# TensorE transposes for the first tokens, a second batch of loads behind them, and a re-weighted order of work in a two-layer attention and FFN kernel

## The chip, the cores and the metric

The kernel runs on one core of one Trainium2 chip. The metric is device time in microseconds. A core has five engines that run their own instruction streams and meet at semaphores: TensorE (PE, matmuls; its weight loads are listed apart as PEld), VectorE (DVE), ScalarE (ACT), GpSimd (POOL) and SyncE (SP, which here only issues DMAs). ACT and POOL issue some DMAs as well.

## The reference

There are 2048 tokens of width 512 in bf16. Two layers follow each other with the same weights; each is an attention block and a gated FFN, both behind a LayerNorm without weights and both added to x:

```python
x = A_x
for _ in range(2):                       # written out in the reference
    x = x + A(layernorm(x), wq, wk, wv, wo, beta)
    x = x + B(layernorm(x), w1, w3, w2)

def A(x):                                # 32 heads of 16; 4 segments of 512 tokens
    q, k, v = x @ wq, x @ wk, x @ wv
    M, z = 0, 0
    for s in range(4):
        p = softmax(qs ks^T / 4 + causal mask)      # within the segment
        a_dot = p vs
        a_mem = (phi(qs) M) / (phi(qs) z + 1e-6)    # phi(t) = t+1 if t>0 else exp(t)
        o = sigmoid(beta) a_mem + (1 - sigmoid(beta)) a_dot
        M, z = M + phi(ks)^T vs, z + sum(phi(ks))
    return o @ wo

def B(x):                                # inner width 1376
    return (silu(x @ w1) * (x @ w3)) @ w2
```

The memory M is carried from segment to segment of a layer. For segment 0 it is zero, so the kernel skips its read there.

## The kernel before

**Work units.** Token tiles have 128 rows, a segment has four of them, and both layers together have eight segments, numbered g = 0 to 7 (g = 4 * layer + s). For a segment, `layer_norm` computes statistics on DVE (L541, L543), the power -0.5 on POOL (L548) and the normalized tile on DVE (L554), and turns each tile with a DMA transpose on SP (L558). `project` makes q and k transposed and v by rows, in twelve jobs of four matmuls (L593, L598); for the first segment q and k are made in two halves of 256 tokens. `attention` runs 20 units of logits (L766), Exp on ACT (L775) and causal masks on POOL (L788); `attend` multiplies by v (L814), copies the result from PSUM to an `xs` buffer and turns it with a DMA transpose (L826). `normalise` scales by the row sums, adds the memory part and transposes once more (L850 to L871). `out_proj` (L879, L883) adds to x, a second `layer_norm` follows, and `ffn` runs the gate and up matmuls (L910), tanh on ACT (L921), two products on DVE (L923, L927) and the down matmuls (L938) with their addition to x (L943). Segment 0 does its attention in two halves of 256 tokens.

`memory_update` forms phi(k)^T v (L657), adds it into `macc` (L663) and masks it into the block-diagonal `mblk` (L665). `memory_read` multiplies phi(q) with it: a denominator (`mden`, L680), its eps, reciprocal and gate on DVE (`mde` L685, L687, L688), and four numerators (`mnum`, L699) that DVE scales to `om` (L703).

**The order.** No order is written out by hand. Every operation is entered with the tiles it reads and writes, the buffers it uses, a priority (smaller goes first) and gates, which are operations that must have been issued before. A planner in the kernel's own Python, `Sched.schedule`, simulates the engines with estimated durations and fixes each engine's instruction order; the engines then run it strictly in that order. For each engine it takes the operations whose predecessors are issued and chooses by these lines:

```python
w = max(tf, s + (R_SLACK if op.mode == "R" else SLACK[e]))
...
lim = max(smin, tf) + LOOK[e]
```

`s` is the time at which the operand is estimated ready, `tf` the time at which the engine is free; among operations whose `w` lies within `LOOK` of the earliest, the smallest priority goes first. So `SLACK` is a margin by which an operand should be ready ahead, and `LOOK` is how far the engine may be kept for something more important. `DMA_SLACK` is an extra margin for DVE and TensorE behind a DMA. An operation that ends with several engines to choose from (`ev`, a copy from PSUM) goes to ACT or DVE, whichever starts first.

**Buffers.** PSUM has two pairs of banks for logits ("S") and four single banks ("B") for everything else. There are three `xs` buffers, eleven large "W" buffers for activations and two for the memory block.

**Head.** Warm-up matmuls on a zeroed buffer (`spin`, L472) keep TensorE running: eight operations, the first two planned as twice as long, 32 matmuls in all. SP and ACT issue the first loads (x tile 0, wq, x tile 2 on SP; x tile 1, wk, x tile 3, wv and beta on ACT). `second_loads` issues x tiles 4 to 7 and four pieces of w1 and w3 on SP behind the last transpose of the first LayerNorm; `late_loads` puts wo, x tiles 8 to 11, w2 and x tiles 12 to 15 on POOL's queue, each at a numbered attention unit of segment 0. `gate_constants` computes sigmoid(beta) by a tanh on ACT.

Of the kernel before, what the change touches and what calls it, by code (L numbers as in the profile page):

```python
# [4 lines left out]
ALU = mybir.AluOpType  # L5
# [22 lines left out]
DMA_SLACK = 800.0  # L28
# [4 lines left out]
SLACK = {"pe": 120.0, "act": 0.0, "dve": 200.0, "pool": 60.0, "sp": 0.0}  # L33
LOOK = {"pe": 90.0, "act": 100.0, "dve": 20.0, "pool": 20.0, "sp": 20.0}
# [29 lines left out]
class Sched:  # L64
# [59 lines left out]
    def schedule(self):  # L124
# [23 lines left out]
        while left:  # L148
# [88 lines left out]
            else:  # L237
# [7 lines left out]
                else:  # L245
                    x0 = max(s + 700.0, dma_free)
# [109 lines left out]
def build(nc, A_x, A_wq, A_wk, A_wv, A_wo, A_beta, B_w1, B_w3, B_w2, out):  # L356
# [33 lines left out]
    xs_r = ring("xs", 3, [P, 512])  # L390
# [11 lines left out]
    bdm = sb("bdm", [P, 8, 17])  # L402
    cm = [sb("cm%d" % i, [P, 1], F32) for i in range(2)]
# [37 lines left out]
    def ev(dst, src, n, **k):  # L441

        def fn(e):
            if hasattr(e, "activation"):
# [11 lines left out]
                                   base=15, channel_multiplier=-1), 136, reads=["bdm"], writes=["bdm"], prio=CP)  # L456
    for ee in range(2):
        dve(lambda e, ee=ee: e.tensor_reduce(cm[ee][:], bdm[:, ee::2, 0], axis=mybir.AxisListType.X, op=ALU.add), 4,
            reads=["bdm"], writes=["cm%d" % ee], prio=CP)
# [6 lines left out]
    WARM = 8  # L466
    if WARM:
        dve(lambda e: e.memset(xs_r[0][:], 0.0), 200, writes=["warm"], prio=CP - 1)

        def spin(e, B=new("B")):  # L470
            for _ in range(4):
                o = e.matmul(bank(B), xs_r[0][:, 0:128], xs_r[0][:], start=True, stop=True)  # L472
            return o
        wb = spin.__defaults__[0]
        pools["xs"].prev[0] = [pe(spin, 4 * MM512 * (2 if i < 2 else 1), reads=["warm"], writes=[(wb, 0)], bufs=[wb], prio=CP, name="warm")
# [22 lines left out]

    def second_loads(first):
        ldw("act", wv_sb, A_wv, "wv", CP + 3)  # L500
        rs = [op for op in S.ops[first:] if op.name == "xT"][-1]

        def early(out_ap, in_ap, size, n, keys, name):
            dma("sp", out_ap, in_ap, size, prio=CP + 4 + n, writes=keys, name=name, gates=[rs], after=[rs])
        early(x_tok[:, 4:8, :], xv[:, 4:8, :], 524288, 0, [("x", 4 + j) for j in range(4)], "ldx")
        for a in range(2):
            for n, (t, src, key) in enumerate(((w1_sb, B_w1, "w1"), (w3_sb, B_w3, "w3"))):
                early(t[:, 2 * a:2 * a + 2, :], src[256 * a:256 * a + 256, :].rearrange("(g p) f -> p g f", p=P), 704512,
                      2 + 2 * a + n, [key + str(a)], "ld" + key)
# [4 lines left out]
    def late_loads():  # L514
        for a in range(2):
            late(wo_sb[:, 2 * a:2 * a + 2, :], A_wo[256 * a:256 * a + 256, :].rearrange("(g p) f -> p g f", p=P), 262144,
                 5 + 2 * a, ["wo%d" % a], "ldwo")
        late(x_tok[:, 8:12, :], xv[:, 8:12, :], 524288, 9, [("x", 8 + j) for j in range(4)], "ldx")
# [5 lines left out]
        late(x_tok[:, 12:16, :], xv[:, 12:16, :], 524288, 18, [("x", 12 + j) for j in range(4)], "ldx")  # L524

    def gate_constants():
        act(lambda e: e.activation(gth[:], betab[:], ACT.Tanh, scale=0.5), 32, False, reads=["betab"], writes=["gth"], prio=0.1)
# [3 lines left out]
            reads=["gth"], writes=["g1"], prio=0.1)  # L531


    def layer_norm(s, name, prio, gates=(), fine=False, part=(0, LT), dst=None):
# [16 lines left out]
        for i in tiles:  # L551
# [5 lines left out]
                bufs=[st, xn], hold=[dst], prio=prio, name="norm")  # L557
            dmaT(lambda e, i=i, xn=xn: e.dma_start_transpose(dt_[dst.slot][:, :, i * 128:(i + 1) * 128], xn_r[xn.slot][:, :]),  # L558
# [4 lines left out]
    def release(g, n):  # L563
# [3 lines left out]
        return units.get((g - 2, 12 + n)) if n < 8 else units.get((g - 1, 2 * (n - 8)))  # L567
# [4 lines left out]
    def project(s, g, X, first):  # L572
# [10 lines left out]
        for n, (kind, Gs, hf) in enumerate(jobs):  # L583
# [36 lines left out]
            elif kind == "k" and Gs[0] == NCG - 1:  # L620
                for pg in range(4):
# [3 lines left out]
                          bufs=[z.k, z.km], prio=g - 1 + 0.3, name="km", gates=[units.get((g - 1, 4))])  # L625
# [17 lines left out]
    def memory_update(g, z, pkb):  # L643
# [5 lines left out]
        for hf in range(2):  # L649
            B = new("B")  # L650

            def fn(e, hf=hf, B=B):
# [11 lines left out]
                reads=[(B, 0), ("macc", hf)], writes=[("macc", hf)], bufs=[B], prio=g - 99.7, name="macc")  # L664
# [3 lines left out]
                375, reads=[("macc", hf), "bdm"], writes=[(mb, hf)], bufs=[mb], prio=g + 0.3, name="mblk")  # L668
        mstate["mb"] = mb

    def memory_read(g, pqb):
# [4 lines left out]
        def fn(e):  # L676
# [9 lines left out]
            writes=[(rm, 0)], bufs=[B, rm], prio=g - 99.9, name="mde")  # L686
# [333 lines left out]
```

## Time and profile before

| | us |
|---|---|
| median of 16 runs | 517.04 |
| lowest and highest of them | 516.23, 521.86 |
| the profiled execution, its own time | 516.87 |
| its span, first to last instruction | 515.1 |

Mean granted TensorE clock over the span: 0.980 of full speed.

How to read what follows. A row of an engine names the line of the kernel, the operation, what it writes and reads, and how many instructions it merges; in square brackets stands the idle time of that engine just ahead and what ended it. A row of stages gives, for each engine, busy time and instructions in brackets. Matmuls of one stream overlap, so the mean duration of one (about 380 ns at 512 columns) is longer than the distance from one to the next (about 215 ns). DMA transposes are issued one after another by SP.

| row of the groups | count | mean ns |
|---|---|---|
| Exp, L775 (ACT) | 180 | 1707 |
| PSUM copy, L445 (ACT) / L446 (DVE) | 55 / 105 | about 600 / 680 |
| mask, L788 (POOL) | 256 | 660 |
| memory numerator matmul 128x128, L699 (PE) | 96 | 223 |
| table load (ACT) | 1 | 1283 |
| DMA transposes of normalized tiles, L558 (SP), issue to landing | 64 | 2500 |

### The profile page before, as it was taken

To read this page: it belongs to the slowest core of one execution; us is meant where nothing else is said; L and a number is where in the kernel's file an instruction comes from. 1 tells how busy PE (TensorE), PEld (TensorE's weight loads), DVE (VectorE), ACT (ScalarE), POOL (GpSimd) and SP (SyncE) were. 2 spreads that over 40 slices of the span, in tenths; PEclk is the share of its full clock that TensorE was granted. 3 is DMA by queue.
4 is the path that set the end of the run, shared out by engine and by line. 5 is a ranking of instruction groups with operands and counts; after the bars stand their busy time and mean duration, and the time that the engine had idled before them with its cause. 6 is when DMAs were issued, how large, how long until landed. Compare 5 with 4: busy or idle time off the path is not lost.

```text
span 515.1 us, 10399 instructions
## 1 busy us (share of the span) xinstructions
PE 486.3 (94%) x4117; PEld 215.8 (42%) x4184; DVE 403.3 (78%) x809; ACT 395.9 (77%) x350; POOL 230.5 (45%) x340
## 2 busy tenths in 40 slices
PE   9978889999999999999799999999999999999997
PEld 4523434654543443334343344433433334444443
DVE  5786999985888798688956899869886597479472
ACT  1998999989978988789977999878988799522130
POOL 1676445564446545555433453454554454310000
PEclk9986999999999999999989999999999999999999
DMA  6969732441142254130531124213322122210201
GB/s 194 280 146 174 144 72 57 68 94 40 33 73 56 49 93 73 31 74 12 98 67 42 41 53 94 62 32 54 84 50 42 42 65 50 73 31 11 72 1 41
DMA packets 108144, 36.91 MB, mean 72 GB/s; under 512 B 101344, under 2 KB 105952, under 8 KB 108096
## 3 DMA queue, kind: packets, MB, share of 16 engines
q1 hardware_dynamic: 105728, 31.94, 30.1%
q0 software_dynamic: 880, 2.98, 2.2%
q10 hardware_dynamic: 1488, 1.32, 0.8%
q8 instruction: 33, 0.54, 0.5%
q14 instruction: 15, 0.12, 0.1%
HBM read 8.43 MB, written 2.10 MB: 20 GB/s over the span
## 4 chain that ended last, share of the span: by engine, by line
PE 66%; DVE 17%; ACT 12%; issue 2%; DMA 1%; POOL 0%
PE psall L910 25%; PE psall L938 15%; ACT e L775 10%; PE psall L766 7%; PE psall L814 6%; PE psall L598 6%; PE psall L879 4%; DVE xn L554 3%; DVE ln L541 2%; PE psall L472 2%; DVE h L927 2%; DVE gp L923 2%; PE psall L593 2%; ACT px L633 1%; DVE x_tok L883 1%
## 5 line engine op out<-in xcount | busy, mean ns | idle before, releaser
L775 ACT ACTIVATE e<-psall 128x2048 bf16<-128x2048 f32 (+1 forms) x180 | 300.8, 1707 | 43.2 <-PE psall L766 42.9
L788 POOL TENSOR_SCALAR_AFFINE_SELECT e<-e 128x512 bf16<-128x512 bf16 x256 | 163.8, 660 | 182.8 <-ACT e L775 181.0
L910 PE MATMUL psall<-W,w 128*128 128x512 bf16 (+3 forms) x768 | 168.6, 357 | 3.7 <-issue 1.6
L910 PEld LDWEIGHTS psall<-W,w 128*128 128x128 bf16 (+1 forms) x792 | 73.9, 100 | 79.0 <-issue 14.0
L921 ACT ACTIVATE th<-psall 128x512 bf16<-128x512 f32 (+2 forms) x89 | 51.9, 594 | 43.7 <-PE psall L910 43.1
L938 PE MATMUL psall<-w,h 128*128 128x512 bf16 (+1 forms) x338 | 83.8, 380 | 1.3 <-issue 0.6
L923 DVE SCALAR_TENSOR_TENSOR gp<-th,psall 128x512 bf16<-128x512 bf16 (+2 forms) x89 | 59.1, 671 | 13.2 <-ACT th L921 13.0
L927 DVE SCALAR_TENSOR_TENSOR h<-gp,psall 128x512 bf16<-128x512 bf16 (+1 forms) x89 | 59.3, 671 | 11.3 <-PE psall L910 11.0
L943 DVE TENSOR_TENSOR x_tok<-psall,x_tok 128x512 bf16<-128x512 f32 x32 | 22.0, 689 | 39.0 <-PE psall L938 39.0
L814 PE MATMUL psall<-e,va 128*32 128x256 bf16 (+3 forms) x1088 | 46.7, 306 | 2.9 <-DVE om L703 1.2
L766 PE MATMUL psall<-W 16*128 16x256 bf16 (+3 forms) x544 | 42.3, 300 | 7.1 <-ACT e L775 6.0
L938 PEld LDWEIGHTS psall<-w,h 128*128 128x128 bf16 (+1 forms) x352 | 31.8, 98 | 38.3 <-issue 6.5
L541 DVE BATCH_NORM_STATS2 ln<-x_tok 128x6 f32<-128x512 bf16 x64 | 42.5, 677 | 1.6 <-DMA x_tok<-in_A_x_dram 1.1
L766 PE MATMUL psall<-W,km 32*128 32x256 bf16 (+3 forms) x544 | 42.1, 299 | 0.1
L446 DVE CAST W<-psall 128x512 bf16<-128x512 f32 x43 | 28.9, 679 | 9.9 <-PE psall L598 9.9
L554 DVE TENSOR_SCALAR xn<-x_tok,ln 128x512 bf16<-128x512 bf16 x64 | 34.7, 573 | 2.3 <-POOL ln L548 1.8
L814 PEld LDWEIGHTS psall<-e,va 128*32 128x32 bf16 x1088 | 24.2, 100 | 28.1 <-issue 8.4
L598 PE MATMUL psall<-W,wq 128*128 128x512 bf16 (+1 forms) x141 | 34.7, 356 | 0.3 <-issue 0.2
L598 PE MATMUL psall<-W,wk 128*128 128x512 bf16 (+1 forms) x139 | 34.4, 356 | 0.3 <-issue 0.2
L766 PEld LDWEIGHTS psall<-W 16*128 16x128 bf16 x544 | 13.2, 92 | 48.9 <-ACT e L775 42.9
L593 PE MATMUL psall<-wv,W 128*128 128x512 bf16 x118 | 32.2, 383 | 1.2 <-issue 1.0
L879 PE MATMUL psall<-wo,W 128*128 128x512 bf16 x117 | 30.4, 388 | 1.1 <-issue 0.8
(61 smaller groups left out, 435.6 us busy)
## 6 DMA issues: line engine op xcount, KB each, us to landing
w<-in_B_w_dram SPq DMA_DIRECT2D x4, 688.0 KB, 8.2
out_dram<-x_tok SPq DMA_DIRECT2D x16, 128.0 KB, 1.7
km<-W SPq DMA_DIRECT2D x24, 64.0 KB, 2.5
w<-in_B_w_dram POOLq DMA_DIRECT2D x3, 384.0 KB, 4.2
W<-xn SPq DMA_TRANSPOSE x64, 2.5
xg<-xs SPq DMA_TRANSPOSE x64, 2.4
x_tok<-in_A_x_dram POOLq DMA_DIRECT2D x2, 512.0 KB, 4.6
W<-og SPq DMA_TRANSPOSE x36, 2.4
```

Source lines behind the costliest of these rows:

```text
L541: dve(lambda e, i=i, tt=tt: e.bn_stats(ln_r[st.slot][:, i, 0:6], x_tok[:, tt, :]), 540, reads=[("x", tt)], writes=[(st, 0, i)], bufs=[st], ...
L598: fn = lambda e, cg=cg, G=G, B=B, st=st, sp_=sp_, w=w, a=a, W=W, c0=c0: e.matmul(bank(B)[:, W * a:W * a + W], w[:, cg, 128 * G:128 * G + 1 ...
L766: o = e.matmul(S4[:, sps(pg), c:c + n], kk[32 * pg:32 * pg + r, G, 128 * j:128 * j + 128], q_r[z.q.slot][32 * pg:32 * pg + r, G, 128 * t1 ...
L775: act(lambda e, N=N, ebuf=ebuf, pgs=pgs, sps=sps: e.activation(e_r[ebuf.slot][:, pgs[0]:pgs[-1] + 1, 0:N], S4[:, sps(pgs[0]):sps(pgs[-1]) ...
L788: pool(lambda e, ebuf=ebuf, c=c: e.affine_select(e_r[ebuf.slot][:, :, c:c + 128], e_r[ebuf.slot][:, :, c:c + 128], pattern=[[0, 4], [1, 128]],
L814: o = e.matmul(bank(X)[32 * pg:32 * pg + 32, base + W - n:base + W], va_r[z.va.slot][:, j, h:h + 32], e_r[eb.slot][:, pg, c:c + n], start= ...
L879: pe(lambda e, i=i, G=G, B=B: e.matmul(bank(B), ot_r[z.ot.slot][:, G, 128 * i:128 * i + 128], wo_sb[:, G, :], start=(G == 0), stop=(G == N ...
L910: prev = pe(lambda e, i=i, cg=cg, ft=ft, B=B, w=w: e.matmul(bank(B)[0:width(ft), W * i:W * i + W], w[:, cg, 128 * ft:128 * ft + width(ft)] ...
L921: act(lambda e, fw=fw, NW=NW, B=B, th=th: e.activation(th_r[th.slot][0:fw, 0:NW], bank(B)[0:fw, 0:NW], ACT.Tanh, scale=0.5), NW, reads=[(B ...
L923: dve(lambda e, fw=fw, NW=NW, B=B, th=th, gp=gp: e.scalar_tensor_tensor(gp_r[gp.slot][0:fw, 0:NW], th_r[th.slot][0:fw, 0:NW], 1.0, bank(B) ...
L927: dve(lambda e, fw=fw, NW=NW, B=B, gp=gps[fg], h=hs[fg]: e.scalar_tensor_tensor(h_r[h.slot][0:fw, 0:NW], gp_r[gp.slot][0:fw, 0:NW], 0.5, b ...
L938: prev = pe(lambda e, ft=ft, fw=fw, B=B, h=h, c=c: e.matmul(bank(B), h_r[h.slot][0:fw, c:c + 128], w2_sb[0:fw, ft, :], start=(ft == 0), st ...
```

## The change

For the first segment alone (`fine`), each normalized tile is turned by four TensorE transposes into one PSUM bank, with an identity matrix that POOL builds, and copied out by ACT or DVE; the four DMA transposes of L558 fall away there. Warm-up becomes nine operations with 18 matmuls in all, and they get the worst priority instead of the best.

All loads of the second batch wait for the last statistics instruction of the first LayerNorm, and are issued on SP: wv (before on ACT, in the first batch), x tiles 4 to 7, w1 and w3 in four pieces, and wo in one piece (before on POOL at units 5 and 7, in two). The load of x tiles 8 to 11 on POOL moves from unit 9 to unit 5. The tanh of beta also waits for unit 2 of segment 0.

Four xs buffers take the place of three. In `release`, the V jobs of later segments wait for units 0, 1, 2, 3 of the segment before instead of 0, 2, 4, 6. LayerNorm of segments 2 and later waits for unit 13 two segments before instead of 10; the four copies that form `km` wait for unit 0 instead of 4. Priorities: `mblk` from g + 0.3 and `mde` from g - 99.9 to g - 300, `macc` from g - 99.7 to g - 95, `mnum` from about g - 800 to g - 400, the copy to xs from about -10000 to g - 100.2, and the FFN's LayerNorm (segment 0 apart) from g + 0.1 to g - 60. The planner's margins and one of its DMA estimates change too. The diff, cut to its core:

```diff
-DMA_SLACK = 800.0
+DMA_SLACK = 500.0
...
-SLACK = {"pe": 120.0, "act": 0.0, "dve": 200.0, "pool": 60.0, "sp": 0.0}
-LOOK = {"pe": 90.0, "act": 100.0, "dve": 20.0, "pool": 20.0, "sp": 20.0}
+SLACK = {"pe": 120.0, "act": 0.0, "dve": 0.0, "pool": 0.0, "sp": 300.0}
+LOOK = {"pe": 90.0, "act": 150.0, "dve": 10.0, "pool": 20.0, "sp": 20.0}
...
-                    x0 = max(s + 700.0, dma_free)
+                    x0 = max(s + 1100.0, dma_free)
...
-    xs_r = ring("xs", 3, [P, 512])
+    xs_r = ring("xs", 4, [P, 512])
...
+    ident = sb("ident", [P, P])
...
+    pool(lambda e: e.memset(ident[:], 1.0), 128, writes=["ident"], prio=CP + 0.5)
+    pool(lambda e: e.affine_select(ident[:], ident[:], pattern=[[1, P]], compare_op=ALU.is_equal, fill=0.0, base=0,
+                                   channel_multiplier=-1), 128, reads=["ident"], writes=["ident"], prio=CP + 0.5)
...
-    WARM = 8
+    WARM = 9
...
-            for _ in range(4):
+            for _ in range(2):
...
-        pools["xs"].prev[0] = [pe(spin, 4 * MM512 * (2 if i < 2 else 1), ..., prio=CP, name="warm")
+        pools["xs"].prev[0] = [pe(spin, 2 * MM512 * (2 if i < 4 else 1), ..., prio=1e4, name="warm")
...
+    def ldx4(q, i, prio, **k):
+        dma(q, x_tok[:, i:i + 4, :], xv[:, i:i + 4, :], 524288, prio=prio, writes=[("x", i + j) for j in range(4)], name="ldx", **k)
...
-        ldw("act", wv_sb, A_wv, "wv", CP + 3)
-        rs = [op for op in S.ops[first:] if op.name == "xT"][-1]
+        k = dict(after=[op for op in S.ops[first:] if op.name == "bnst"][-1:])
+        k["gates"] = k["after"]
+        dma("sp", wv_sb[:], A_wv.rearrange("(g p) f -> p g f", p=P), 524288, prio=CP + 3, writes=["wv"], name="ldwv", **k)
+        ldx4("sp", 4, CP + 6, **k)
...
+        dma("sp", wo_sb[:], A_wo.rearrange("(g p) f -> p g f", p=P), 524288, prio=CP + 12, writes=["wo"], name="ldwo", **k)
...
-        for a in range(2):
-            late(wo_sb[:, 2 * a:2 * a + 2, :], ..., 262144, 5 + 2 * a, ["wo%d" % a], "ldwo")
-        late(x_tok[:, 8:12, :], xv[:, 8:12, :], 524288, 9, [("x", 8 + j) for j in range(4)], "ldx")
+        ldx4("pool", 8, CP + 5, gates=[units[(0, 5)]], after=[units[(0, 5)]])
...
+            if fine:
+                B = new("B")
+                tb = lambda B=B: bank(B).bitcast(BF16)[:, 0:512].rearrange("p (g c) -> p g c", g=NCG)
+
+                def turn(e, xn=xn, tb=tb):
+                    for cg in range(NCG):
+                        o = e.transpose(tb()[:, cg, :], xn_r[xn.slot][:, 128 * cg:128 * cg + 128], ident[:])
+                    return o
+                pe(turn, 4 * 62, reads=[(xn, 0), "ident"], writes=[(B, 0)], bufs=[B, xn], prio=-900, name="xt")
+                ev(lambda i=i: dt_[dst.slot][:, :, i * 128:(i + 1) * 128], tb, 512, reads=[(B, 0)], writes=[(dst, i)],
+                   bufs=[B, dst], prio=-900, name="evt")
+                continue
...
-        return units.get((g - 2, 12 + n)) if n < 8 else units.get((g - 1, 2 * (n - 8)))
+        return units.get((g - 2, 12 + n)) if n < 8 else units.get((g - 1, n - 8))
...
-                          bufs=[z.k, z.km], prio=g - 1 + 0.3, name="km", gates=[units.get((g - 1, 4))])
+                          bufs=[z.k, z.km], prio=g - 1 + 0.3, name="km", gates=[units.get((g - 1, 0))])
...
-                reads=[(B, 0), ("macc", hf)], writes=[("macc", hf)], bufs=[B], prio=g - 99.7, name="macc")
+                reads=[(B, 0), ("macc", hf)], writes=[("macc", hf)], bufs=[B], prio=g - 95.0, name="macc")
...
-                375, reads=[("macc", hf), "bdm"], writes=[(mb, hf)], bufs=[mb], prio=g + 0.3, name="mblk")
+                375, reads=[("macc", hf), "bdm"], writes=[(mb, hf)], bufs=[mb], prio=g - 300, name="mblk")
...
-            writes=[(rm, 0)], bufs=[B, rm], prio=g - 99.9, name="mde")
+            writes=[(rm, 0)], bufs=[B, rm], prio=g - 300.0, name="mde")
...
-            pe(fn2, ..., hold=[om], prio=g + 0.12 + 0.1 * G - 800, name="mnum")
+            pe(fn2, ..., hold=[om], prio=g + 0.12 + 0.1 * G - 400, name="mnum")
...
-        ev(lambda: xs_r[xs.slot][:], ..., prio=pr * 0.01, name="evX")
+        ev(lambda: xs_r[xs.slot][:], ..., prio=g - 100.2, name="evX")
...
-            X = layer_norm(s, "xa", g - 1.0, gates=[units.get((0, 5)) if g == 1 else units.get((g - 2, 10))], fine=(g == 0))
+            X = layer_norm(s, "xa", g - 1.0, gates=[units.get((0, 5)) if g == 1 else units.get((g - 2, 13))], fine=(g == 0))
...
+                gth_op.gates.append(units[(0, 2)])
...
-                layer_norm(s, "xf", -300.0 if g in HALVES else g + 0.1, part=part, dst=X2)
+                layer_norm(s, "xf", -300.0 if g in HALVES else g - 60, part=part, dst=X2)
```

## The prediction

> **What bounds the kernel now.** I read the page's first two parts, then the busy time stage by stage, then the instructions in order of time at the two places where TensorE stands still.
>
> ```profile
> PE 486.3 (94%) x4117; PEld 215.8 (42%) x4184; DVE 403.3 (78%) x809; ACT 395.9 (77%) x350; POOL 230.5 (45%) x340
> ...
> PE   9978889999999999999799999999999999999997
> ...
> PEclk9986999999999999999989999999999999999999
> ```
>
> TensorE is busy 486.3 of 515.1 us, and the two dents of its row are dents of its granted clock too. The stages:
>
> ```profile
> 0.00:10.70 10.70, 9.44 (x32) 3.71 (x33) 6.53 (x21) 1.51 (x2) 2.57 (x9) 1.00 0.75 221
> ...
> 30.00:60.00 30.00, 23.57 (x265) 9.52 (x271) 23.66 (x61) 27.80 (x30) 18.45 (x28) 0.77 0.83 168
> 60.00:110.00 50.00, 45.32 (x478) 24.21 (x483) 48.09 (x101) 45.90 (x42) 26.47 (x38) 1.00 0.38 73
> 110.00:250.00 140.00, 135.86 (x1191) 60.16 (x1210) 112.98 (x224) 123.00 (x102) 74.59 (x107) 1.00 0.30 57
> 250.00:260.00 10.00, 6.46 (x88) 3.09 (x88) 8.48 (x17) 8.43 (x9) 3.60 (x6) 0.78 0.51 92
> 260.00:450.00 190.00, 185.28 (x1555) 76.86 (x1583) 148.14 (x286) 158.99 (x127) 89.19 (x131) 0.99 0.27 57
> 450.00:515.00 65.00, 61.19 (x279) 28.07 (x283) 41.32 (x73) 13.13 (x22) 3.03 (x3) 1.00 0.11 31
> ```
>
> Columns: stretch, length, then busy time of PE, PEld, DVE, ACT, POOL, then granted clock, DMA share, GB/s. Up to 10.7 us TensorE runs only warm-up matmuls. From 14.6 to 60 ACT sets the pace with segment 0's Exp (15.36 of 15.40 us, then 27.80 of 30); from 60 to 110 DVE does (48.09 of 50); after that TensorE is 97% busy, and from 450 on it works off a backlog of FFN matmuls with ACT nearly idle. So the end is: TensorE's fixed work plus what it loses before and between. What it loses: the head, 6.4 us idle and a clock of 0.77 in 30 to 60, 4.7 us in 60 to 110, 3.5 us idle and a clock of 0.78 in 250 to 260, some 9 us spread over the rest.
>
> **The head.** The instructions in order of time (start, length):
>
> ```profile
> 1.26 9.62 PE L472 MATMUL psall<-xs 128*128 128x512 bf16 x32 [1.26 <-DVE mhalf L451]
> ...
> 6.28 0.73 DVE L554 TENSOR_SCALAR xn<-x_tok,ln 128x512 bf16<-128x512 bf16 x2 [0.82 <-POOL ln L548]
> ...
> 6.72 6.64 SPq L558 DMA_TRANSPOSE W<-xn  x4
> 7.89 1.29 DVE L541 BATCH_NORM_STATS2 ln<-x_tok 128x6 f32<-128x512 bf16 x2 [0.87 <-DMA x_tok<-in_A_x_dram]
> ...
> 10.72 1.04 PE L598 MATMUL psall<-W,wq 128*128 128x256 bf16 x8
> ```
>
> The second normalized tile is ready at 7.01, the first projection starts at 10.72: 3.7 us are the DMA transpose. The change puts four TensorE transposes and one PSUM copy in its place. The trace has no transpose; its nearest row is the memory read's matmul with the same 128x128 operands (L699), four in 0.41 us. The PSUM copy took 0.60 on ACT, 0.68 on DVE. So 7.01 + 0.41 + 0.65 + 0.2 for three hand-offs (0.03 to 0.1 each here) = 8.3: 2.4 us earlier. Eighteen warm-up matmuls instead of 32 must also be out of the way: the first twelve follow each other by 0.43, the rest by 0.21, so they end near 1.26 + 5.1 + 1.3 = 7.7. They now have the worst priority, so transposes may go ahead of them; if all go first, the start is 8.8. I take **-2.2**, from -2.4 to -1.9.
>
> Here a rule speaks against the change. The Trainium skill, "VectorE: DVE Perf Modes", section "The three transpose paths", prices a 128x128 transpose at 390 ns on TensorE and 1309 on the DMA. Both agree with the DMA row (1.3 us an issue on SP), but eight times 390 in sequence is 3.1 us: from 6.7 to 9.8, 10.4 with the copy, a gain of 0.3 only. I go by the row, since matmuls of one shape overlap here (four of 223 ns in 0.41 us); 390 reads as the length of a single one. The page's sum stays as the far end.
>
> A second rule: "TensorE: Matmul & The Clock Gate", section "The HAM clock gate (the 'warmup' mystery)", says about 3.4 us of sustained work lifts the clock and a similar idle window drops it. This trace lifts it later, at about 6.4 us, 5.1 after the first matmul. With either number 18 matmuls suffice and the gap to 8.3 is short; if the clock stayed halved, the first projections (3.4 us of them before the first logits) would cost up to 3.4 more. I take 0.
>
> ACT: the table load (1.28 us, at 3.40) stood before the beta tanh, which now waits for unit 2. The first ACT operation becomes a PSUM copy. A load in front of it runs in ACT's idle time before 7; one between the copies and the first Exp would cost 1.28. I take 0. The 16 transposes are 1.6 us of TensorE at most, inside the head; the four copies 2.4 us on ACT and DVE, which idle there; memset and mask of the identity on POOL, about 0.2 and 0.4 by the bdm rows, end before 3.
>
> **The loads.** Without wv in the first batch 0.52 MB less precedes x tiles 2 and 3 (about 1.4 us at 380 GB/s), so their statistics move from 7.9 to near 6.7 and end near 8. Then SP issues wv, x 4 to 7, four w1/w3 pieces, wo: 7 x 0.4 us; SP has nothing else before the first attention transpose (22.05 now). wv of 0.52 MB lands 3.5 to 6.9 us after issue (the four such loads), so at 12 to 15; V is computed from 14.89 now, 12.7 after the shift. If V stands first on TensorE, the logits behind it wait and ACT with them: 0 to 2 us, I take **+0.3**. For x 4 to 7 there are some 5 us of margin (landing by 18, statistics at 23.6), for w1/w3 over 60 (first use 92.5). All of SP's bytes, 4.3 MB at 395 GB/s, are in at about 21, against an attention transpose issued at 19.9; now it is 24 against 22.05. POOL loses wo's two issues (0.91, 0.73 us) and makes the one of x 8 to 11 (0.80) about 7 us earlier, among masks. In 24 to 46 the DMA engines are full and an oT transpose takes 5.33 us to land (40.50 on the chain), so 0.5 MB less there shortens the chain from first-half attention to its output projection. I take **-0.5** for 30 to 60, from -4 (a third of the 13 us lost there) to +1.
>
> **The memory step.** At 250 to 260, where the memory of layer 1's second segment is updated and read, TensorE stands:
>
> ```profile
> 251.39 0.68 PE L657 MATMUL psall<-va,W 128*128 128x136 bf16 x8 [0.65 <-DVE va L446]
> ...
> 252.99 0.58 PE L680 MATMUL psall<-mb,W 128*128 128x8 bf16 x16 [0.56 <-DVE macc L663]
> ...
> 254.81 0.41 PE L699 MATMUL psall<-mb,W 128*128 128x128 bf16 x4 [0.83 <-DVE rm L685]
> ...
> 256.85 2.33 PE L814 MATMUL psall<-e,va 128*32 128x512 bf16 x32 [1.22 <-DVE om L703]
> ```
>
> These four waits are 3.3 us, and the clock falls for some 13 us: 0.22 of the 6.5 busy us before 260 and 0.12 of the 9.9 after are 2.6. DVE is working all along: macc, then a gp (0.60) before mblk, phmin, mde, reciprocal (0.95), then four om for four mnum matmuls that hold PSUM banks. The change lifts mblk and mde above everything else on DVE and lowers mnum from -800 to -400, behind projections. The rest of the chain is as long as before. I expect half: **-2.8** at this place, from -5.9 to +1. Elsewhere the memory matmuls show some 4 us of idle (their groups' 2.2 + 0.6 + 3.2, less 2.0 here), most of it for V's copies and the FFN; nothing taken.
>
> **Order and buffers.** From segment 2 on, LN waits for unit 13 two segments before, not 10; at about 2.8 us a unit (20 in some 57 us) that is 8 us later for its DVE steps and its four SP transposes, while its q jobs are released at unit 12 as before. Covered by FFN backlog after 110; before it, by nothing: a late LN leaves TensorE idle. Against that, the FFN's own LN rises from g+0.1 to g-60. The fourth xs buffer lets a PSUM copy run before an older transpose is done; DVE's waits for xs are small (1.7 us), so 0. V's gates and km's four SP copies come up to four units earlier, behind other SP transposes of 1.3 us; SP has room after 110 (DMA share 0.3). DVE's planning margin falls from 200 to 0 ns: operations go into the queue at the instant they are planned ready, and each that is late holds DVE. SP's rises to 300. I take **+0.8** for all this, from -3 to +8.
>
> **Sum:** -2.2 + 0.3 - 0.5 - 2.8 + 0.8 = -4.4 us on a span of 515.1. The profiled execution took 516.87, 0.17 under the median of 517.04 and 1.8 over its span; with the same surroundings the forecast is 517.04 - 4.4 = **512.6**.
>
> **Rivals.** (a) *The early hole fills.* If the shift and the quieter DMA give TensorE segment 1's projections and the first output projection before 46, 4 of the 13 us in 30 to 60 come back, besides more of 250 to 260: 508. For it: oT's 5.33 us. Against it: ACT is 93% busy there, and TensorE's work follows ACT's.
> (b) *No change.* The head's gain is given back where LN starts three units late or at V: 517. For it: DVE-bound 60 to 110, where an earlier start is worth nothing if DVE's order gets worse by 2 us. That the transposes themselves save nothing also ends here.
> (c) *Slower.* DVE blocks at its head because its margin is gone. Place: 60 to 110 and the memory reads, where DVE is 96% busy and has no slack to catch up. Price: 0.6 to 1.2 us for a blocked step (the four waits above), ten more of them 9 us, a second fall of the clock 2.6, less head and loads -2.4, no gain at 250: about +9, so 526; half of it 521. It decides when such waits exceed the 5 us gained elsewhere, six or so. For it: the DVE rows already wait 13.0 us for tanh and 11.0 for matmuls. Against: after 110 TensorE's backlog hides most of DVE's waits.
>
> **Chances.** Main case 0.48 (own range 509 to 516), (a) 0.20, (b) 0.12, (c) 0.20. What a measurement of this kernel can tell from no change is about 0.2%, 1.0 us. Faster: nearly all of the main case, (a), a quarter of (b): 0.70. Same: half of (b) and an edge of the main case: 0.08. Slower: 0.22. Range: low end past (a)'s 508 to 506, high end into (c) to 521; beyond them perhaps 1 in 20 below and 3 in 20 above.
>
> **What would show it.** Right: first L598 matmul near 8.3 and first Exp near 12.3 (14.64 now); one table load; no wait for wv above 0.5 us; a clock of 1.0 and under 2 us idle around the memory read of layer 1's second segment; TensorE idle in the first 110 us lower by some 3. Wrong: first projection after 10 (transposes as dear as the page says), a halved clock at 8 to 12, TensorE waiting for V with the Exps stopped, DVE waits of 1 us in front of gp, h and om in 60 to 110, or a second dent in the clock later on.

## The result and the profile after

| | before | after |
|---|---|---|
| median, us | 516.85 (48 runs) | 510.25 (9 runs) |
| lowest and highest of after | | 507.77, 512.67 |
| ratio, 95% interval | | 0.9862 (0.9842 to 0.9882) |
| profiled execution, its time and its span | 516.87, 515.1 | 509.76, 508.0 |
| mean granted clock | 0.980 | 0.983 |

The kernel became faster by 1.4%, 7.1 us (0.0138 x 517; the ratio is to runs of the kernel before that were timed beside it, the two medians differ by 6.6). The nine runs form two groups that go with the granted clock of each: four of 507.8 to 508.2 us at 0.990, five of 510.3 to 512.7 at 0.979 to 0.987; the profiled execution (0.983) is nearer the second. The page's first two parts, of the kernel after:

```profile
PE 480.3 (95%) x4121; PEld 215.7 (42%) x4186; DVE 404.9 (80%) x807; ACT 390.1 (77%) x340; POOL 239.1 (47%) x356
...
PE   8978998899999999999899999999999999999997
...
PEclk9977999999999999999899999999999999999999
```

There is nearly as much work as before (TensorE has 14 warm-up matmuls less and 16 transposes more). What changed is the dents: the second one, in the middle, is shallower in PE's row (8 for 7), and lies a slice earlier in the clock's. The stages of the kernel after, columns as in the prediction (length, then busy time of PE, PEld, DVE, ACT, POOL, clock, DMA share, GB/s):

```profile
0.00:10.70 10.70, 8.60 (x48) 4.80 (x49) 6.89 (x21) 2.91 (x4) 2.92 (x11) 1.00 0.56 177
...
30.00:60.00 30.00, 24.03 (x277) 10.77 (x282) 22.85 (x58) 26.66 (x31) 16.26 (x26) 0.77 0.72 136
60.00:110.00 50.00, 45.33 (x482) 26.35 (x485) 46.39 (x102) 43.98 (x42) 29.17 (x43) 1.00 0.43 73
110.00:250.00 140.00, 135.64 (x1185) 59.30 (x1204) 116.49 (x227) 120.64 (x98) 73.22 (x106) 0.99 0.35 62
250.00:260.00 10.00, 9.78 (x99) 4.79 (x99) 10.00 (x25) 8.80 (x7) 5.25 (x9) 1.00 0.08 16
260.00:450.00 190.00, 184.44 (x1561) 76.10 (x1588) 148.62 (x284) 157.50 (x124) 96.33 (x140) 1.00 0.30 59
450.00:515.00 65.00, 54.02 (x246) 24.65 (x249) 37.44 (x67) 10.74 (x18) 3.04 (x3) 1.00 0.10 27
```

TensorE's busy time at 250 to 260 is 9.78 of 10 us in place of 6.46, but the stage no longer holds the same work: the memory read of g = 5 now starts at 240.3 (shown below). Its stage after is

```profile
240.00:250.00 10.00, 8.41 (x91) 3.53 (x89) 8.46 (x15) 7.49 (x7) 3.95 (x7) 0.83 0.38 80
```

so TensorE still stands for 1.6 us there in place of 3.5, and the clock still falls: it is halved for 3.4 us, from 243.7, in place of 6.8 us, from 255.6. In 60 to 110 its busy time is unchanged (45.33 against 45.32), but there is more in it: busy time is a poor measure where short and long matmuls mix. So I worked out another quantity for every kernel, the **lost time of TensorE**. All weight loads are in the traces, so each counts as its matmul's share of TensorE at full clock: 0.216 us for 512 columns and 0.109 for 256, the spacing of such matmuls in a row, 0.0335 for one of the packed logits and attention matmuls, and 0.06 or 0.027 for the memory's; warm-up and transposes count 0. That makes some 426 us in every kernel. Lost time at t is t less the value of all loads started before t; it holds waits, a lowered clock and the warm-up alike. Each column is one profiled execution. The first column is before's; the others are differences to it, in us:

```
t    before  after a_loads a_headold  b_turn b_mem b_consts b_look  a_noturn a_nomem a_consts a_ln a_other a_look
10    10.0   -1.9   -1.0     +0.0      -1.2  +0.0   +0.0    +0.0     +0.0    -1.5    -0.9   -1.4  -1.5   -1.4
30    14.4   -0.5   -0.3     -0.2      -0.2  -0.2   -0.2    -0.2     +5.0    -0.5    -0.2   -0.5  -0.5   -0.5
60    29.4   -2.2   -2.7     -0.7      -1.9  -0.7   -2.4    -0.9     +4.8    -2.3    -0.2   -2.0  -3.1   -2.0
70    31.5   -3.6   -4.1     -2.1      -1.5  -1.1   -2.0    -0.4     +5.4    +1.5    -0.6   -3.0  -4.5   -3.1
110   39.8   -3.4   -3.4     -2.6      -0.4  -1.0   +1.3    +0.1     +6.4    +0.9    -0.1   +2.4  -1.7   -0.3
240   55.3   -4.6   -4.4     -4.4      -0.6  -1.7   +4.2    -0.2     +7.1    -0.1    -0.9   +2.3  -2.6   -1.5
270   64.4   -8.0   -8.5     -8.2      -0.4  -1.5   +4.3    -0.6     +5.4    -0.7    -1.3   +2.7  -3.9   -1.3
500   85.3   -6.7   -5.8     -6.7      +1.3  -2.2   +4.7    -0.6     +7.6    +0.0    -0.6   +3.0  -1.3   -0.9
```

The kernel after loses 2.2 us less up to 60, 1.2 less from 60 to 110, 1.2 less up to 240, 3.4 less from 240 to 270, and 1.3 more after that.

**The head after**, the instructions in order of time:

```profile
1.26 5.76 PE L476 MATMUL psall<-xs 128*128 128x512 bf16 x18 [1.26 <-DVE mhalf L452]
...
2.75 1.28 ACT L446 ACT_TABLE_LOAD   x1 [2.75 <-issue]
...
6.10 0.74 DVE L558 TENSOR_SCALAR xn<-x_tok,ln 128x512 bf16<-128x512 bf16 x2 [0.82 <-POOL ln L552]
...
6.86 0.61 PE L568 MATMUL psall<-ident,xn 128*128 128x128 bf16 x8
7.24 0.69 DVE L545 BATCH_NORM_STATS2 ln<-x_tok 128x6 f32<-128x512 bf16 x1 [0.40 <-DMA x_tok<-in_A_x_dram]
7.28 0.60 ACT L446 ACTIVATE W<-psall 128x512 bf16<-128x512 bf16 x1 [3.25 <-PE psall L568]
7.85 0.41 DVE L447 COPY W<-psall 128x512 bf16<-128x512 bf16 x1
7.96 0.38 SPq L437 DMA_DIRECT2D wv<-in_A_wv_dram  x1
...
8.31 1.05 PE L614 MATMUL psall<-W,wq 128*128 128x256 bf16 x8 [0.85 <-DVE W L447]
...
12.48 12.94 ACT L791 ACTIVATE e<-psall 128x1024 bf16<-128x1024 f32 x14 [0.18 <-PE psall L782]
...
12.95 0.81 PE L609 MATMUL psall<-wv,W 128*128 128x512 bf16 x3
```

Eight transposes take 0.61 us together, the projection starts at 8.31 and the Exps at 12.48, 2.4 and 2.2 us earlier than before. V has no wait in front of it. The memory read of g = 5 after:

```profile
240.33 0.59 PE L696 MATMUL psall<-mb,W 128*128 128x8 bf16 x16
240.92 0.41 PE L715 MATMUL psall<-mb,W 128*128 128x128 bf16 x4
...
241.90 0.82 PE L895 MATMUL psall<-wo,W 128*128 128x512 bf16 x3 [0.57 <-DVE rm L701]
...
244.15 2.32 PE L830 MATMUL psall<-e,va 128*32 128x512 bf16 x32 [0.77 <-DVE om L719]
...
247.23 2.32 PE L895 MATMUL psall<-wo,W 128*128 128x512 bf16 x10 [0.21 <-issue]
```

It starts 12.7 us earlier, and output-projection matmuls (L895) lie between its steps, where before there were none. The waits shown are 1.6 us together, for 3.3 before.

### The profile page after: what moved, and what is told of

It is laid out like the page before. It is cut to its first block, busy times and chain, and to the rows that moved or that the text cites. A ratio compares the mean times of both kernels' runs of the same rounds, so it can differ in the third digit from the quotient of the medians.

```text
span 508.0 us, 10421 instructions
## 1 busy us (share of the span) xinstructions
PE 480.3 (95%) x4121; PEld 215.7 (42%) x4186; DVE 404.9 (80%) x807; ACT 390.1 (77%) x340; POOL 239.1 (47%) x356
## 4 chain that ended last, share of the span: by engine, by line
PE 68%; DVE 19%; ACT 5%; DMA 4%; issue 3%; POOL 1%; ACTq 0%; SPq 0%; DVEq 0%
PE psall L926 24%; PE psall L954 14%; PE psall L614 7%; PE psall L782 7%; PE psall L830 6%; PE psall L895 4%; ACT e L791 4%; PE psall L609 3%; DVE W L447 2%; DMA W<-xn 2%; DVE W L653 2%; DVE ln L545 2%; DVE xn L558 1%; DVE gp L939 1%; DVE h L943 1%
## 5 line engine op out<-in xcount | busy, mean ns | idle before, releaser
L954 PE MATMUL psall<-w,h 128*128 128x512 bf16 (+1 forms) x334 | 82.5, 380 | 1.6 <-issue 0.8
L830 PE MATMUL psall<-e,va 128*32 128x256 bf16 (+3 forms) x1088 | 45.5, 306 | 1.0 <-DVE om L719 0.8
L447 DVE CAST xs<-psall 128x512 bf16<-128x512 f32 x50 | 32.7, 680 | 13.4 <-PE psall L830 13.2
L447 DVE CAST W<-psall 128x512 bf16<-128x512 f32 x47 | 31.6, 680 | 10.3 <-PE psall L614 9.8
L614 PE MATMUL psall<-W,wq 128*128 128x512 bf16 (+1 forms) x140 | 35.3, 360 | 3.1 <-DMA W<-xn 0.9
L558 DVE TENSOR_SCALAR xn<-x_tok,ln 128x512 bf16<-128x512 bf16 x64 | 31.8, 534 | 3.3 <-POOL ln L552 3.2
```

The lines of the kernel that those rows point to most:

```text
L447: return e.tensor_copy(dst(), src())
L614: fn = lambda e, cg=cg, G=G, B=B, st=st, sp_=sp_, w=w, a=a, W=W, c0=c0: e.matmul(bank(B)[:, W * a:W * a + W], w[:, cg, 128 * G:128 * G + 1 ...
L830: o = e.matmul(bank(X)[32 * pg:32 * pg + 32, base + W - n:base + W], va_r[z.va.slot][:, j, h:h + 32], e_r[eb.slot][:, pg, c:c + n], start= ...
L954: prev = pe(lambda e, ft=ft, fw=fw, B=B, h=h, c=c: e.matmul(bank(B), h_r[h.slot][0:fw, c:c + 128], w2_sb[0:fw, ft, :], start=(ft == 0), st ...
```

## The experiments

Ratios are to the kernel before, timed beside each; 0.001 is 0.5 us. Kernels named b_ start from the kernel before, those named a_ from the changed one. Since the planner makes a new order for every edit, I also compared the orders: TensorE's weight loads in order of time, merged into runs that load for the same matmuls, and of these runs (kind and length) the share that two kernels have in common in the same order.

### One part on the kernel before

**The transposes.** The kernel before with the identity, the TensorE transposes and the short warm-up; its second batch of loads waits for the last transpose.

```diff
+            if fine:
...
+                pe(turn, 4 * 62, ..., prio=-900, name="xt")
...
-        rs = [op for op in S.ops[first:] if op.name == "xT"][-1]
+        rs = [op for op in S.ops[first:] if op.name == "xt"][-1]
```

> The kernel before with the TensorE transposes, the identity and the shorter warm-up alone; loads as before, except that the second batch waits for the last TensorE transpose in place of the last DMA transpose. Theory 1 (the parts act where they are put): first projection near 8.3 us in place of 10.72, first Exp near 12.4, and the end earlier by 1.3 to 2.4 us, so 514.5 to 515.5. Rival (the transposes need the loads moved too, since x tiles 2 and 3 still wait behind wv): first projection near 8.3 but the end earlier by under 1 us. Rival (order noise): anything within 3 us of before, with the memory step at 250 us changed as well.

Ratio 0.9996 (0.9981 to 1.0012): nothing. The first projection starts at 8.99, ahead of before's 10.72:

```profile
8.99 1.05 PE L614 MATMUL psall<-W,wq 128*128 128x256 bf16 x8 [0.95 <-ACT W L446]
```

The lost time is 1.9 us lower at 60, 0.4 at 110 and 0.6 at 240. So the head's gain is given back in 60 to 110, where DVE set the pace before and where the memory read of g = 1 lies: it loses 6.5 us here, 4.9 before (table further below). The order isn't quite before's either.

**The memory priorities.**

```diff
-... prio=g - 99.7, name="macc")
+... prio=g - 95.0, name="macc")
-... prio=g + 0.3, name="mblk")
+... prio=g - 300, name="mblk")
-... prio=g - 99.9, name="mde")
+... prio=g - 300.0, name="mde")
-... prio=g + 0.12 + 0.1 * G - 800, name="mnum")
+... prio=g + 0.12 + 0.1 * G - 400, name="mnum")
```

> The kernel before with the four priorities of the memory step alone (macc, mblk, mde, mnum). Theory 1: the 3.3 us of TensorE waits around 250 us and the fall of the clock go, 2.8 to 3.4 us earlier, 513.5 to 514. Rival 2 (the planner's margins removed that stall): within 1 us of before, and the stall still there.

Ratio 0.9969 (0.9955 to 0.9983), -1.6 us: a gain, but not at 240 to 270, where the difference in lost time hardly moves (-1.7 to -1.5), and the clock is halved for 6.8 us as before. The read of g = 5 still stops TensorE:

```profile
250.61 0.41 PE L699 MATMUL psall<-mb,W 128*128 128x128 bf16 x4 [0.83 <-DVE macc L663]
...
254.36 0.61 PE L766 MATMUL psall<-W 16*128 16x384 bf16 x8 [1.98 <-ACT e L775]
```

**The planner's margins.**

```diff
-DMA_SLACK = 800.0
+DMA_SLACK = 500.0
-SLACK = {... "dve": 200.0, "pool": 60.0, "sp": 0.0}
+SLACK = {... "dve": 0.0, "pool": 0.0, "sp": 300.0}
-LOOK = {... "act": 100.0, "dve": 20.0, ...}
+LOOK = {... "act": 150.0, "dve": 10.0, ...}
-                    x0 = max(s + 700.0, dma_free)
+                    x0 = max(s + 1100.0, dma_free)
```

> The kernel before with the planner's constants alone (DMA_SLACK, SLACK and LOOK of ACT, DVE, POOL and SP, the DMA's start estimate). Theory 1: between no change and 2 us slower, since DVE loses its margin. Rival 2 (the re-weighted planner is where the gain lies): 2 to 4 us faster, with the stall at 250 us gone.

Ratio 1.0072 (1.0049 to 1.0096), +3.7 us. The place is 60 to 240: the lost time goes from -2.4 at 60 to +1.3 at 110 and +4.2 at 240. The stage of this kernel:

```profile
60.00:110.00 50.00, 41.72 (x452) 22.37 (x451) 44.93 (x91) 44.25 (x39) 22.77 (x32) 1.00 0.39 67
```

TensorE is busy 3.6 us less than before in these 50 us and DVE 3.2 us less, so DVE isn't overloaded there, it stands: the waits that the trace lists for it there are 4.8 us, 1.8 before, the longest (1.6) for V's matmuls. That fits rival (c), at its place and at some 4 of its 9 us. But nearly half of the order is another one too, so the margins aren't shown to be the cause of all of it.

**A control.** TensorE's LOOK from 90 to 100 ns, an edit with no meaning of its own.

```diff
-LOOK = {"pe": 90.0, ...}
+LOOK = {"pe": 100.0, ...}
```

> A control: the kernel before with the planner's LOOK of TensorE at 100 in place of 90, a step that is in no part of the change. Theories 1 and 2: the same to within 1 us. Rival 3 (order noise: any new order moves the end by some us): 2 us or more either way, with the stall at 250 us in another shape.

Ratio 0.9997 (0.9986 to 1.0008). But here the order hardly changes (0.98 of the runs match), so this control bounds little. b_turn's order matches before's to 0.77, b_mem's to 0.68, b_consts' to 0.57, the changed kernel's to 0.37.

### One part taken back from the changed kernel

**The transposes, with the new loads kept.** DMA transposes and the warm-up of before.

```diff
-            if fine:
+            if False:
-    WARM = 9
+    WARM = 8
```

> The changed kernel with the first tiles turned by DMA transposes again and the long warm-up of before; the loads stay in their new place, so the last two transposes stand on SP behind 4.3 MB of loads. Theory 1 (parts add; transposes alone gave nothing before): 0 to 2.5 us slower than the changed kernel, 510.5 to 513. Rival 4 (the early start is kept only where the rest of the order can use it, which the changed kernel's can): 2 to 5 us slower, 512.5 to 515, the deficit of TensorE carried from 15 us to the end.

Ratio 1.0137 (1.0119 to 1.0154), +7.1 us, the slowest of all. SP's queue of this kernel, by issue time and time taken:

```profile
10.55 2.07 SPq L437 DMA_DIRECT2D w<-in_B_w_dram  x4
12.66 0.53 SPq L437 DMA_DIRECT2D wo<-in_A_wo_dram  x1
13.31 6.40 SPq L574 DMA_TRANSPOSE W<-xn  x2
```

The transposes of x tiles 2 and 3 stand behind seven loads (wv, x tiles 4 to 7 and the five above) and take 6.4 us to issue. V's first matmuls come at 14.78, as before (14.89), but q and k of the second half of segment 0 only at 28.08, before at 17.27, and ACT has no Exp from 25.9 to 35.3:

```profile
25.40 0.63 PE L609 MATMUL psall<-wv,W 128*128 128x512 bf16 x1 [0.66 <-DMA W<-xn]
...
28.08 1.46 PE L614 MATMUL psall<-W,wq 128*128 128x256 bf16 x6
```

The same projection in the kernel before:

```profile
17.27 0.38 PE L598 MATMUL psall<-W,wq 128*128 128x256 bf16 x2
```

At 30 us 5.0 us more are already lost than before. So the early loads need TensorE's transposes. The other way round is not so: the next run keeps the transposes and takes the early loads back.

**The loads.** The second batch and the late loads of before; the batch waits for the last TensorE transpose.

```diff
-        k = dict(after=[op for op in S.ops[first:] if op.name == "bnst"][-1:])
+        ldw("act", wv_sb, A_wv, "wv", CP + 3)
+        rs = [op for op in S.ops[first:] if op.name == "xt"][-1]
-        dma("sp", wo_sb[:], ..., name="ldwo", **k)
+            late(wo_sb[:, 2 * a:2 * a + 2, :], ..., 5 + 2 * a, ["wo%d" % a], "ldwo")
```

> The changed kernel with the loads of before (wv from ACT in the first batch, x 4 to 7, w1, w3 on SP behind the last TensorE transpose, wo in two pieces on POOL at units 5 and 7, x 8 to 11 at unit 9). Theory 1: 0.5 to 1.5 us slower than the changed kernel, 511 to 512. Rival 4: 2 to 4 us slower, because x tiles 2 and 3 and the first attention transposes come later, lost before 60 us and not won back.

Ratio 0.9859 (0.9838 to 0.9881), the same as the changed kernel. TensorE's order is identical, so this is a clean comparison: the loads are worth nothing in time, to within some 1.5 us by the two intervals. In this execution the clock doesn't fall at the read of g = 5, whose loss is 4.1 us in place of 5.4: with one order, that much comes and goes with the clock.

**The memory priorities** (the four lines of b_mem, the other way round).

> The changed kernel with the memory step's four priorities of before. Theory 1: slower by what they gave alone, 1.6 us, at 250 us, so about 512. Rival 4 (together with DVE's lost margin they matter more): 3 to 5 us slower, with a stall of TensorE at the memory steps and a second fall of the clock.

Ratio 1.0006 (0.9993 to 1.0019): the whole gain is gone. Most of it goes at the **first** read, g = 1: from 60 to 70 us this kernel turns -2.3 into +1.5, and is then 5.1 us behind the changed kernel. A further 2.8 are lost against it in 240 to 270. The instructions at the first read:

```profile
64.21 0.59 PE L696 MATMUL psall<-mb,W 128*128 128x8 bf16 x16 [0.76 <-DVE va L447]
...
66.26 0.60 PE L715 MATMUL psall<-mb,W 128*128 128x128 bf16 x4 [0.79 <-DVE rm L701]
...
69.28 1.91 PE L895 MATMUL psall<-wo,W 128*128 128x512 bf16 x4 [1.56 <-DVE om L719]
```

The clock falls here as well, halved for 6.8 us from 66.0. The changed kernel passes the same place without a wait:

```profile
63.40 0.58 PE L696 MATMUL psall<-mb,W 128*128 128x8 bf16 x16
64.04 0.38 PE L614 MATMUL psall<-W,wq 128*128 128x512 bf16 x1
```

**The margins** (the lines of b_consts, the other way round).

> The changed kernel with the planner's constants of before. Theory 1 (parts add; the constants alone cost 3.8 us): 2 to 4 us faster than the changed kernel, 506 to 508, and so better than both. Rival 4 (the constants fit only the changed order): 1 to 4 us slower, 511 to 514, most of it between 60 and 110 us.

Ratio 0.9962 (0.9948 to 0.9976): the changed kernel with the old margins is 5.2 us slower than with the new ones, while the new ones alone cost 3.7 on the kernel before. Either the sign of this edit depends on what it meets, or one or both figures belong to the new order and not to the margins; the control below leaves that open.

### The head alone, and the rest of the order

**The head and the loads of before in the changed order.** a_loads, with `if False` for the transposes and the warm-up of before; the batch waits for the last DMA transpose.

> The changed kernel with the head of before: DMA transposes of the first tiles, the long warm-up, and the loads of before, so that no load stands in front of a transpose on SP (in the run without TensorE transposes two of them stood behind 4.3 MB). Order, margins and buffers as changed. If the head is worth its 2.2 us and the rest of the gain lies in the order: 512 to 513.5. If the order after 60 us only works from an early start: 515 or more. If the head is worth nothing: 510 to 511.

Ratio 0.9903 (0.9875 to 0.9931). Its order matches the changed kernel's to 0.97, and the differences lie ahead of 54 us, so it shows the head in nearly one order: a_loads and the changed kernel, 0.9859 and 0.9862, are 2.2 us faster. With the three intervals taken as independent that is 2.2 ± 1.6 us; the profiled spans, 508.5 and 508.0, show only 0.5, and the two columns of lost time meet again by 240. And it shows that **-5.0 of the -7.1 us need neither the early head nor the new loads**.

**LayerNorm's gate and priority.**

```diff
-... units.get((g - 2, 13))], fine=(g == 0))
+... units.get((g - 2, 10))], fine=(g == 0))
-                layer_norm(s, "xf", -300.0 if g in HALVES else g - 60, part=part, dst=X2)
+                layer_norm(s, "xf", -300.0 if g in HALVES else g + 0.1, part=part, dst=X2)
```

> The changed kernel with the LayerNorms ordered as before (next segments' from unit 10, the FFN's at g + 0.1). If the lift of the FFN's LayerNorm and the later start of the next ones are what removes the loss of DVE's margin: 2 to 5 us slower, 512 to 515. If the memory priorities do that alone: within 1 us of the changed kernel.

Ratio 1.0024 (1.0007 to 1.0041). The loss is in 70 to 110: -3.0 becomes +2.4.

**All other edits of the order**: those of a_ln, three xs buffers, and before's gates of V and km and priority of the copy to xs.

```diff
-    xs_r = ring("xs", 4, [P, 512])
+    xs_r = ring("xs", 3, [P, 512])
-... units.get((g - 1, n - 8))
+... units.get((g - 1, 2 * (n - 8)))
-... name="km", gates=[units.get((g - 1, 0))])
+... name="km", gates=[units.get((g - 1, 4))])
-... prio=g - 100.2, name="evX")
+... prio=pr * 0.01, name="evX")
```

> The changed kernel with everything of before except the head, the loads, the memory priorities and the constants: three xs buffers, V's, km's and LayerNorm's gates, the copy to xs and the FFN's LayerNorm as before. If those small edits matter no more than their own waits did (1.7 us of DVE waiting for xs): within 1.5 us of the changed kernel, 509 to 511.5. If the gain needs all of them together: 513 to 518.

Ratio 0.9956 (0.9937 to 0.9976). More edits are taken back than in a_ln, and it is faster by 3.5 us. The effects don't add.

**The control again**, LOOK of TensorE from 90 to 100 ns on the changed kernel.

> A control at the changed kernel: LOOK of TensorE at 100 in place of 90, in no part of the change. If the gain rests on what the edits do: within 1 us of the changed kernel, 509 to 511. If the changed order is one lucky order among many: 2 us or more slower, 512.5 or above.

Ratio 0.9961 (0.9943 to 0.9979), **5.1 us slower than the changed kernel** by an edit without a meaning. This time the order is another one: 0.53 of the runs match. a_nomem, a_consts, a_ln, a_other and a_noturn match to 0.40 to 0.47. So what each loses against the changed kernel (7.4, 5.2, 8.4, 4.9 us for the first four) can't be put down to the edit taken back: this one draw of another order costs 5.1. By their intervals a_nomem and a_ln lie beyond the control, by 2.3 and 3.3 us, but one control is one draw; a part of their own is possible for these two, not shown.

Part of the 5.1 goes with the clock. The mean granted clock of a_look's twelve runs is 0.978, of the changed kernel's nine 0.985, and among these nine 0.001 goes with 0.35 us; by that rate the difference is worth some 2.5 us, an estimate.

### What the orders have in common

For each kernel, TensorE's lost time from 10 us before the denominators to 10 after, at the reads of g = 1 and g = 5; when the second starts; and how many output-projection matmuls TensorE has from 5 us before it to 12 after:

```
            g=1   g=5   start  o-proj
before      4.9   8.2   253.0    0
b_look      5.3   8.0   252.9    0
b_turn      6.5   8.2   252.5    0
b_mem       4.3   6.7   245.1    8
b_consts    7.4   8.4   256.9    0
a_noturn    5.5   7.9   265.2    0
a_nomem     8.3   6.9   256.3    0
a_consts    5.6   7.9   256.9    0
a_ln        2.0   8.0   255.3    0
a_other     1.8   6.9   245.0   12
a_look      1.2   8.0   252.3    0
after       2.6   5.4   240.3   16
a_loads     2.6   4.1   240.6   16
a_headold   2.6   4.1   240.9   16
```

The read at g = 5 loses 7.9 to 8.4 us with no output projection beside it (6.9 in a_nomem), 6.7 to 6.9 with 8 or 12 of its matmuls and 4.1 to 5.4 with 16. Two things limit this. The three kernels with 16 have one order, so they are one draw. And b_mem's stall lies partly outside these 20 us: counted 15 us to either side it loses 9.1, before 8.8, a_other 7.6, the three with 16 5.2 to 6.5. So the small loss goes with that order and its output projection; that these matmuls are the cause isn't shown. The clock goes along: it is halved at this read for 6.8 us in before and a_look, for 3.4 after, not at all in a_loads and a_headold. a_look has every edit of the change and still stops there:

```profile
250.89 0.39 PE L782 MATMUL psall<-W 16*128 16x512 bf16 x4 [0.87 <-ACT e L791]
...
252.34 0.59 PE L696 MATMUL psall<-mb,W 128*128 128x8 bf16 x16 [0.44 <-DVE gp L939]
...
256.69 0.40 PE L782 MATMUL psall<-W 16*128 16x256 bf16 x4 [1.98 <-ACT e L791]
```

At g = 1 the loss is 1.2 to 2.6 us in six kernels, all with the new memory priorities and the new margins (a_headold, with the old head, among them), and 4.3 to 8.3 in the others: without the priorities 8.3, without the margins 5.6, with the priorities alone 4.3, with the margins alone 7.4. a_noturn has both and still loses 5.5; there the second half of segment 0 is late. So both edits together go with a small loss here, in orders that match the changed kernel's to as little as 0.40. How much of it needs the margins is less sure: counted 15 us to either side the six lose 3.6 to 5.1 and b_mem, with the priorities alone, 4.9, before 6.1.

## Why the prediction was right or wrong

The forecast was 512.6 with a range of 506 to 521; the time was 510.25. Direction and range were right; the gain was 7.1 us (by the ratio) in place of 4.4. That it came out no farther off is partly luck: with 10 ns more in one planning constant the same edits give 2.0 us (a_look).

**The head, -2.2: right in its timing, nearer to conditional in its worth.** First projection at 8.3, 8.31 measured; first Exp at 12.3, 12.48. The sum met 8.3 with two of its terms off: DVE's copy took 0.41 us for 0.65, but began only at 7.85, behind the statistics of the next x tile. The rest: one table load, at 2.75, in ACT's idle time; the statistics of x tiles 2 and 3 began at 7.24 for 6.7. The transposes settled the question between row and rule: 219 ns each, the row's 223, but eight in 0.61 us. The Trainium skill, "VectorE: DVE Perf Modes", section "The three transpose paths", at 390 each in sequence would have made 3.1. Its DMA figure did not agree with the row, as I had it: it is for 128x128, and SP's 1.3 us are the issue alone of a 128x512 tile, which landed after 2.4 to 3.2. The step that the timing doesn't prove is that the shift passes to the end one to one. On the kernel before it was worth 0.0 (b_turn: 0.2 us, within the interval), given back in 60 to 110, the place that rival (b) named. In the new order 2.2 ± 1.6 us remained.

**The clock, 0: right, with little to spare.** At 8 to 12 the first eight projection matmuls take 1.05 us, as before (1.04). The 1.00 of the stage up to 10.7 proves nothing: the kernel before has it too, though its first twelve matmuls follow each other by 0.43 us and the later ones by 0.21. In a_loads the faster spacing came only at 7.21, with three of the 18 warm-up matmuls left.

**The loads, +0.3 and -0.5: both nothing.** The wv load landed 4.0 us after its issue at 7.96, and V was computed at 12.95 without a wait. The quieter DMA in 30 to 60 (share 0.72 for 0.83) gave nothing either: a_loads has the old loads, 0.5 us less lost time at 60, and the same end.

**The memory step, -2.8: met in size (8.2 to 5.4 us at the read, -3.4 in 240 to 270), but the reason was wrong in part.** I put it down to `mblk` and `mde` going first on DVE. b_mem has just that and the stall stays; a_look has it and the stall stays. It is smaller only in the order that brings 16 output-projection matmuls to the read. Of the signs, TensorE's idle time there came true (1.6 us), the clock of 1.0 did not in the profiled execution (halved for 3.4 us). Before, it was halved for 6.8 us, not lowered for some 13 as I read it; the loss of 2.6 us stands. What the priorities go with most is the read at g = 1, which I had left out ("nothing taken").

**Order and buffers, +0.8: the failed step.** I priced the edits one by one as risks, and saw no gain. a_headold has all of them with the memory edits and gives -5.0, where the sum for both had -2.0. In the lost time the surplus lies in 60 to 110 (-1.2) and 110 to 240 (-1.2). The lowered margins, which I feared as rival (c), came with a loss of 3.7 us alone on the kernel before and are part of the best order.

**The rivals.** (a) came true to a smaller part: 1.7 us of the 15.0 lost in 30 to 60 came back, not 4, at an unchanged clock of 0.77. (b) is what happened to the head alone. (c) fits what happened to the margins alone, at less than half its price.

**What stays open.** The control shows that about 5 of the 7 us lie in one particular order. a_loads and a_headold, with the loads or the head of before, come to it as well; the other six variants of the changed kernel do not (514.9 to 524.3 us). Which edit, if a single one, leads to that order isn't settled by these runs, since each of the others taken back changes the whole order. Nor is it settled why the clock falls at the read of g = 5 in some orders and executions and not in others.

## What to carry to other kernels

Where a planner fixes the order, run a control that changes the order without meaning anything before you credit an edit: here 10 ns in one planning constant were worth 0.2 us on one kernel and 5.1 on the other, as much as two of the edits taken back. An edit is measured cleanly where the order stays (a_loads, a_headold), and what it saves at the start can be gone 60 us later (b_turn), so follow the saving to the end. Before you reorder loads on a queue, look which small transfers on it others wait for: the same early loads cost nothing with TensorE's transposes, and held up the next projections by 11 us with DMA transposes behind them.

## What the hardware showed unexpectedly

- TensorE's warm-up matmuls went from a spacing of 0.43 us to 0.21 at different times under one and the same warm-up: the first weight load at the faster spacing is at 6.36 us in the kernel before and at 4.12 in b_consts, 5.1 and 2.9 us after the first matmul.

```profile
6.36 1.65 PEld L472 LDWEIGHTS psall<-xs 128*128 128x128 bf16 x8 [0.28 <-issue]
4.12 3.77 PEld L472 LDWEIGHTS psall<-xs 128*128 128x128 bf16 x18 [0.17 <-issue]
```

  The Trainium skill, "TensorE: Matmul & The Clock Gate", section "The HAM clock gate (the 'warmup' mystery)", has about 3.4 us of sustained work for this; the two lie on both sides of it.
- After the clock has risen it falls for stretches of like length: in the 14 traces it is halved, ahead of the last 10 us, for 3.4, 6.8, 10.2, 13.7 or 17.1 us at a time, multiples of 3.4. In 30 to 60 it is 13.7 us before and after alike.
- DVE copied a 128x512 tile from PSUM in 0.42 us where PSUM held bf16 and in 0.68 where it held f32; ACT took 0.60 for the bf16 tile, as for f32 before.

```profile
L447 DVE CAST W<-psall 128x512 bf16<-128x512 f32 x47 | 31.6, 680 | 10.3 <-PE psall L614 9.8
L447 DVE COPY W<-psall 128x512 bf16<-128x512 bf16 x2 | 0.8, 416 | 0.9 <-PE psall L568 0.9
```

- A DMA transpose of a normalized tile took 1.2 to 1.3 us to issue on SP in the first LayerNorm of the kernel before, and 5.1 in a_noturn right behind the seven loads; from issue to landing it was 2.4 to 3.2 us before and up to 11.6 there.
